# w_out as float32r through GpSimd transfers, the column mean straight from it, one operation to scale and centre, and log w in pairs, in a new order

## Chip, cores, metric

One core of one Trainium2 chip. The metric is the device time of one launch in microseconds (us), median over runs. The kernel before takes 151.41 us (three runs, 151.08 to 151.83). Where two kernels are compared, the ratio is the mean time of one kernel's fast runs over the mean of the other's fast runs of the same rounds, with a 95% interval; so it is not quite the ratio of the medians quoted beside it. A run counts as slow when it is over 1.5% above the fastest of the same kernel, and is then left out of the ratio, though not out of the median. "Loss" below is (ratio - 1) times the median of the kernel before in those rounds.

## The reference, cut

```python
for t in range(S):                       # attention: batch 4, 8 heads, 768 tokens, 48 wide
    cur = einsum('bhd,bhe->bhde', u * k[t], v[t])
    y[t] = einsum('bhd,bhde->bhe', r[t], state + cur)
    state = w[t][..., None] * state + einsum('bhd,bhe->bhde', k[t], v[t])
x = y.reshape(3072, 384)
h = x @ w_in                             # 384 x 1024
solu = h * softmax(h)
ln = (solu - mean(solu)) / sqrt(var(solu) + 1e-6) * g_ln
out = ln @ w_out                         # 1024 x 384
```

The mean of the layer norm is folded into the weights: with w = g * w_out (row by row), `(solu - mean) @ w` equals `solu @ (w - column mean of w)`. So w_out is scaled by g and centred once, at the start. That set-up is what the change is about.

## The kernel before

The sequence is cut into 24 units of 128 tokens. Every engine executes its own instructions strictly in the order of one list of words. A word is a step, a unit (or block) number and, where there is a choice, an engine: a = ACT (ScalarE), v = DVE (VectorE), g = GpSimd. The words used below: `ldw`, `ldk`, `ldr`, `ldv` load a unit (192 KB each, in pieces of 192 B); `ldwin`, `ldwout` load the weights; `lw` is log w, `cum` its cumulative sums, `kp`, `kt`, `kr`, `M`, `m` lead to the scores, `dg`, `dv` to the diagonal term, `Y`, `y` the attention output, `X`, `xT` its transpose; `H` is x @ w_in (h_ps), `e` the exponential, `he` = h * e, `hq` its square, `Oa`, `Ob` the product with w_out (o_ps). The set-up has `gw` (scale w_out by g), `mean`, and `wt` (centre); `dm` is a warm-up matmul.

```python
wout_f = consts.tile([128, KF, DM], F32)                       # KF = 8 blocks of 128 x 384
def load_w_out(half):                                          # ldwout: on the SyncE queue
    part = slice(half * KF // 2, (half + 1) * KF // 2)
    sp.dma_start(out=wout_f[:, part, :], in_=wout_v[:, part, :])
...
def setup_gain(f, engine):                                     # gw
    if engine is act:
        act.activation(out=gw[:, f, :], in_=wout_f[:, f, :], func=COPY, scale=gr[:, f:f + 1])
    else:
        engine.tensor_scalar(out=gw[:, f, :], in0=wout_f[:, f, :], scalar1=gr[:, f:f + 1], scalar2=None, op0=MULT)

def setup_mean():                                              # mean: eight bf16 matmuls
    for f in range(KF):
        pe.matmul(m_ps, lhsT=mean_w, rhs=gw[:, f, :], start=(f == 0), stop=(f == KF - 1))

def setup_w2(f, engine):                                       # wt: all eight on GpSimd
    engine.tensor_add(out=w2[:, f, :DM], in0=gw[:, f, :], in1=mean_sb)
...
def log_w(i):
    act.activation(out=L["lw"][:, :, :D], in_=L["w"], func=LN)
```

The list, from the last loads of w_out to the first output matmuls (cuts marked):

```
... m2v dv1v ldwout0 dm4 p2g Y1 q2g S1 y1v ldwout1 qa2 gw1a gw0a dm2 X1 xT0v xT1v dg2 H0 H1 ldw3 e0 st1 S0 dm13 ldv2 gw4v gw6v
gw3g he0 ldk3 gw5a ... gw7a ldr3 e1 ldk4 lw3 gw2g mean mean_sb:a vb2g ldw5 dv2g he1 Y2 ldr4 cum3 wt2g y2v exp3 lw4 et3 p3v
hq0a wt3g cum4 wt1g X2 dm0 wt0g ... wt4g kp3 S2 kt3 ... wt7g ... wt6g ldr6 Oa0 kp4 p4v exp5 wt5g ...
```

The softmax here doesn't subtract the row's maximum and nothing guards it: scores larger than these inputs give would overflow.

Of the kernel before, what the change touches and what calls it, by code (L numbers as in the profile page):

```python
# [14 lines left out]
SQUARE = mybir.ActivationFunctionType.Square  # L15
IDENTITY = mybir.ActivationFunctionType.Identity
# [8 lines left out]
dm5 dm3 dm18 dm1 ldw0 ldr0 small dm16 dm8 ldk0 lw0 ldw1 ldr1 cum0 exp0 et0 lw1 rows cum1 ldk1 p0g ldw2 kp0 exp1 ubc kt0 p1g kr0v ldr2 M0 ldk2 ldv0 et1  # L25
kp1 lw2 m0a q0g kt1 kr1v ldwin2 cum2 q1g sel0 dg0 exp2 M1 dm10 et2 vb0a kp2 m1a ldwin1 ldv1 kt2 win2a dg1 dv0g kr2v win1a vb1a Y0 y0v sel1 ldwin0 M2
win0a dm6 X0 m2v dv1v ldwout0 dm4 p2g Y1 q2g S1 y1v ldwout1 qa2 gw1a gw0a dm2 X1 xT0v xT1v dg2 H0 H1 ldw3 e0 st1 S0 dm13 ldv2 gw4v gw6v gw3g he0 ldk3
gw5a dm12 dm17 ldw4 st0 gw7a ldr3 e1 ldk4 lw3 gw2g mean mean_sb:a vb2g ldw5 dv2g he1 Y2 ldr4 cum3 wt2g y2v exp3 lw4 et3 p3v hq0a wt3g cum4 wt1g X2 dm0
wt0g ldk5 dm9 ldr5 exp4 lw5 ldw6 wt4g kp3 S2 kt3 ldv3 cum5 st2 ldw7 wt7g ldv4 et4 kr3a xT2v wt6g ldr6 Oa0 kp4 p4v exp5 wt5g M3 q3v et5 m3a kt4 kr4v
ldk6 Oa1 kp5 hq1a H2 M4 q4g kt5 Ob0 ldv5 sel3 ldw8 lw6 vb3a e2 dg3 kr5a dv3g m4v sq0a dg4 vb4g dv4g p5g vb5g Ob1 ldr7 M5 lw7 ldk7 Y3x ldv6 he2 m5v qm0  # L30
q5g p6g y3a cum6 X3 xT3v sq1v Y4 qm1 exp6 y4v H3 lv0 lv1 et6 ldr8 X4 hq2v ldk8 kp6 Oa2 dg5 o0a xT4a dv5g p7g sto0 ldw9 S4 e3 S3 st4 st3 q6g H4 Y5 vb6g
q7g ldr9 o1a he3 kt6 lw8 S5 Ob2 e4 ldk9 y5v cum7 ldr10 he4 kr6a st5 X5 hq3a sq2a exp7 M6 Oa4 ldv7 ldk10 ldr11 Oa3 qm2 m6v cum8 ldv8 qa6 et7 xT5a sto1
dg6 ldr12 ldk11 lv2 kp7 qa7 Ob3 dv6g exp8 p8g ldw10 p9v kt7 et8 o2a dg7 sq3g kp8 H5 qm3 q8g hq4a lv3 ldv9 e5 ldw11 Y6x kr7v ldv10 p10g M7 vb7g o3v Ob4
ldw12 kt8 m7v y6a q10g lw9 X6 sq4v he5 cum9 xT6a qm4 ldk12 exp9 kr8a dg8 et9 dv7g Y7 hq5g H6 e6 sto2 kp9 Oa5 ldw13 kt9 y7v lv4 X7 dg10 q9g Ob5 kr9a
he6 vb8g ldv11 ldk13 dv8g ldr13 sq5a o4a M8 ldw14 hq6g m8v S7 M9 qm5 vb10g xT7a p11g ldv12 m9v lv5 Oa6 H7 dg9 st7 lw10 Y8 o5a e7 cum10 vb9g ldw15
exp10 Ob6 y8v he7 sq6g X8 sto3 et10 dv9g S6 kp10 ldk14 xT8a lw12 S8 q11g H8 lw11 lw13 cum11 st8 e8 dv10g st6 Oa7 qm6 kt10 Y9x p12g exp11 hq7v kr10a
lv6 Ob7 y9a he8 M10 et11 S9 ldw16 sto4 o6a ldr14 X9 xT9a kp11 cum12 qa11 Oa8 ldr15 exp12 hq8g m10v p13g ldv13 vb11g ldk15 st9 H9 sq7v et12 qm7 kt11
q12g ldv14 lw14 ldr16 kp12 ldk16 lv7 e9 Y10x q13g sto5 y10a o7v ldk17 kr11v he9 cum13 exp13 ldv15 et13 dg11 kt12 kp13 Ob8 X10 sto6 M11 kr12a sq8g Oa9
qa12 ldk18 dv11g ldr17 dg13 M12 m12v kt13 ldw17 vb12g xT10a qm8 S10 m11a sel11 H10 kr13v M13 lw15 st10 ldv16 hq9a Y11x lv8 p15g e10 y11a m13v vb13g
sto7 o8a Ob9 dg12 p14g ldr18 ldv17 sq9v dv12g p16g X11 ldw18 cum14 xT11a S11 he10 Y12 H11 exp14 S12 qm9 st11 y12v lv9 et14 kp14 q14g dv13g st12 hq10g  # L40
o9a ldv18 e11 Y13 X12 cum15 xT12a ldr19 he11 exp15 kt14 Oa10 y13v sto8 hq11g kr14a vb15a q15g lw16 S13 H12 vb14g et15 ldk19 kp15 e12 dg14 X13 M14 p17g
dv14g kt15 ldw19 m14v xT13a he12 kr15a Ob10 H13 q17g sto9 hq12g sq10a st13 M15 Y14 m15v ldv19 qm10 lv10 vb16g Oa11 e13 lw18 q16g S14 lw17 o10v y14v
cum16 he13 ldw20 exp16 dg15 et16 hq13v Ob11 dv15g X14 kp16 Oa12 p18g sq11a p19g xT14a st14 qm11 lv11 H14 Ob12 o11a e14 cum17 q19g kt16 sq12v ldk20 Y15
sto10 he14 exp17 q18g qm12 Oa13 sto11 kr16a et17 hq14g y15v cum18 kp17 lv12 Ob13 M16 ldr20 ldk21 o12v exp18 dg17 X15 vb17g sq13v kt17 m16a et18 qm13
Oa14 xT15v kp18 kr17v sel16 lv13 H15 o13a lw19 dg16 e15 kt18 M17 dv17g dv16g vb19g ldv20 kr18v m17a lw20 Ob14 Y16 he15 M18 y16v sq14v S16 qm14 dg18
cum19 X16 ldv21 hq15g xT16v m18a exp19 Oa15 H16 ldw21 sel17 S15 dg19 lv14 o14a et19 kp19 Y17 lw21 ldr21 st16 e16 cum20 sel18 vb18g st15 y17v exp20
Ob15 sto12 ldk22 ldr22 X17 sto13 kt19 sq15v ldv22 xT17a he16 dv18g Y18 qm15 kr19a dv19g kp20 p20v y18v hq16g H17 M19 Oa16 lv15 X18 q20g Ob16 m19v o15a
e17 xT18a ldw22 lw22 p22g cum21 sq16v he17 qm16 p21g dg20 ldw23 hq17g ldv23 exp21 Y19 kt20 H18 vb20g ldr23 Oa17 lv16 y19v kp21 q21g kr20v o16a cum22
e18 he18 dv20g kt21 exp22 Ob17 kr21a M20 X19 sq17g S17 qm17 m20a lv17 kp22 qa21 sel20 lw23 S18 xT19v sto14 o17a st17 hq18g M21 Oa18 ldk23 m21v kt22
cum23 H19 sto15 st18 exp23 kr22v vb21a kp23 dg21 dv21g sto16 Y20 Y21 vb22a M22 q22g S19 e19 m22a vb23g y20v X20 p23v st19 he19 q23g Ob18 kt23 xT20a  # L50
sq18v H20 qm18 kr23a sel22 M23 y21v lv18 o18a X21 dg22 hq19v xT21v Oa19 m23a dv22v dg23 sel23 Y22 Ob19 y22v e20 he20 H21 dv23g Y23 sto17 X22 sq19a
Oa20 y23v X23 qm19 lv19 hq20g o19a xT22v e21 xT23v H22 e22 he21 Ob20 sto18 hq21g sq20a qm20 lv20 H23 he22 Oa21 Oa22 sto19 Ob21 e23 hq22g sq21a o20v
qm21 lv21 Ob22 he23 hq23v Oa23 sto20 sq22v sq23a qm22 o21v Ob23 sto21 lv22 qm23 Oc23 o22v sto22 lv23 dm14 oz23v dm15 o23a stz23 dm7 sto23 dm11 dm19
# [25 lines left out]
def kernel(  # L79
# [12 lines left out]
    nc = tc.nc  # L92
# [25 lines left out]
    def load(name, src):  # L118
        def stage(i):
            c, b = units[i]  # L120
            L = live[i]
            if name in "kr":

                if "k_and_r" not in L:
                    L["k_and_r"] = io.tile([C, 2, H, 64], F32, tag="kr_in", name="kr_in")
                t = L["k_and_r"][:, "kr".index(name)]
            else:
                t = io.tile([C, H, 64], F32, tag=name + "_in", name=name + "_in")
            L[name] = t[:, :, :D]
            sp.dma_start(out=L[name], in_=src[b, :, c * C:(c + 1) * C, :].rearrange("h t d -> t h d"))  # L130
        return stage
# [6 lines left out]
    wout_f = consts.tile([128, KF, DM], F32)  # L138
# [9 lines left out]
    def load_w_out(half):  # L148
        part = slice(half * KF // 2, (half + 1) * KF // 2)
        sp.dma_start(out=wout_f[:, part, :], in_=wout_v[:, part, :])  # L150
# [3 lines left out]
    nc.gpsimd.memset(uti_neg, -1.0)  # L154
    nc.gpsimd.affine_select(out=uti_neg, in_=uti_neg, compare_op=ALU.is_ge, fill=0.0, base=0,
                            pattern=[[1, C]], channel_multiplier=-1)
    uts = consts.tile([C, C], BF16)
    nc.gpsimd.memset(uts, 1.0)
    nc.gpsimd.affine_select(out=uts, in_=uts, compare_op=ALU.is_gt, fill=0.0, base=0,
                            pattern=[[1, C]], channel_multiplier=-1)  # L160
    ident = consts.tile([C, C], BF16)
    make_identity(nc, ident)
# [12 lines left out]
    lw_t = [consts.tile([C, H, 64], BF16, name=f"lw{j}") for j in range(NR)]  # L175
    kp_t = [consts.tile([C, 2, H, 64], BF16, name=f"kp{j}") for j in range(NR)]
    for j in range(NR):
        nc.vector.memset(lw_t[j][:, :, D:], 0.0)
        nc.vector.memset(kp_t[j][:, :, :, D:], 0.0)
# [7 lines left out]
    mean_w = consts.tile([128, 128], BF16)  # L187
    nc.vector.memset(mean_w, -1.0 / DF)
    nc.vector.memset(w2[:, :, DM:], 1.0 / RDF)

    ident_f = consts.tile([KF, KF], F32)
    make_identity(nc, ident_f)
# [4 lines left out]
    gw = consts.tile([128, KF, DM], BF16)  # L197
# [9 lines left out]
    def setup_rows_copy():  # L207
        dve.tensor_copy(out=u_bc.rearrange("t h d -> t (h d)"), in_=live[0]["u_ps"])
        dve.tensor_scalar(out=gr, in0=live[0]["g_ps"], scalar1=RDF, scalar2=None, op0=MULT)

# [15 lines left out]
    def setup_gain(f, engine):  # L226
        if engine is act:
            act.activation(out=gw[:, f, :], in_=wout_f[:, f, :], func=COPY, scale=gr[:, f:f + 1])
        else:
            engine.tensor_scalar(out=gw[:, f, :], in0=wout_f[:, f, :], scalar1=gr[:, f:f + 1], scalar2=None, op0=MULT)  # L230

    def setup_mean():
        m_ps = small.tile([128, DM], F32, tag="s", name="mean_ps")
        for f in range(KF):
            pe.matmul(m_ps, lhsT=mean_w, rhs=gw[:, f, :], start=(f == 0), stop=(f == KF - 1))
        live[0]["mean_ps"] = m_ps

    def setup_mean_copy(engine):
        copy(engine, mean_sb, live[0]["mean_ps"])

    def setup_w2(f, engine):
        engine.tensor_add(out=w2[:, f, :DM], in0=gw[:, f, :], in1=mean_sb)


    def log_w(i):
        L = live[i]
        L["lw"] = lw_t[i % NR]
        act.activation(out=L["lw"][:, :, :D], in_=L["w"], func=LN)
# [337 lines left out]
    def part(stage, j):  # L586
# [9 lines left out]
        ldw=load("w", w), ldk=load("k", k), ldr=load("r", r), ldv=load("v", v), ldwin=load_w_in, ldwout=load_w_out,  # L596
# [43 lines left out]
```

## Time and profile before

| | run profiled first | the same kernel again |
|---|---|---|
| time of that run | 156.91 us (slow) | 152.29 us (single run, state unknown) |
| first h_ps | 20.06 us | 20.01 us |
| first o_ps | 30.92 us | 29.67 us |
| first gw on w_out | 21.07 us | 19.80 us |
| first gw on its second half | 23.87 us | 21.88 us |
| matmuls from 85 to 105 us | 270 | 339 |

A line of the timeline: start, length, engine, operation, result <- inputs, size, how many, then in brackets the idle time before and what ended it. Two lines of its timeline (start, length, engine, operation, result <- inputs, size, how many, then in brackets the idle time before and what ended it):

```profile
19.80 1.12 ACT L71 ACTIVATE gw<-wout_f,gr 128x384 bf16<-128x384 f32 x2 [1.33 <-DMA wout_f<-in_moe_w_out_dram]
25.67 7.74 POOL L71 TENSOR_TENSOR w<-gw,mean_sb 128x384 bf16<-128x384 bf16 x8 [0.56 <-ACT mean_sb L71]
```

w_out kept ACT waiting for 1.33 us, and centring took GpSimd 7.74 us in one piece.

### The profile page before, as it was taken

Reading aid. Unit: us, or ns where it says so; the run is one execution under the profiler, and the core shown is the slowest. Engines: PE = TensorE matmul, PEld = TensorE weight load, DVE = VectorE, ACT = ScalarE, POOL = GpSimd, SP = SyncE. Lnnn points to the kernel's source line nnn. Section 1 sums busy time; section 2 is a strip of 40 time slices with the busy share of each in tenths; the row PEclk is TensorE's granted clock in tenths of the full one; section 3 lists DMA queues with packets and bytes.
Section 4 is the critical chain, followed back from the end, with each engine's and each line's share of the span. In section 5 each row is a group of like instructions: output and inputs, shape, how many; then the busy total and the mean of one; then the engine's idle time right before and its main releaser. Section 6 shows DMA issues by size and latency. Waiting matters only on the chain.

```text
span 155.2 us, 5295 instructions
## 1 busy us (share of the span) xinstructions
PE 140.4 (90%) x2156; PEld 109.7 (71%) x2156; DVE 129.4 (83%) x231; ACT 120.2 (77%) x232; POOL 123.1 (79%) x152
## 2 busy tenths in 40 slices
PE   6877897699999899999999799939999999999993
PEld 2344584477786787888788587737888778889771
DVE  7546738899998898999976989999889999998661
ACT  4456767989898979798989698829899888895742
POOL 3375965997999799999947999977799899976800
PEclk9999999999999999999999999999999999999999
DMA  4999997989999999899796999999989311011013
GB/s 95 201 185 301 380 303 152 213 160 190 208 202 184 204 229 187 194 205 233 154 205 157 218 217 200 228 250 180 215 196 211 100 51 55 2 55 55 18 62 127
DMA packets 104970, 27.09 MB, mean 175 GB/s; under 512 B 100329, under 2 KB 104562, under 8 KB 104946
## 3 DMA queue, kind: packets, MB, share of 16 engines
q1 hardware_dynamic: 104946, 26.75, 76.4%
q8 instruction: 17, 0.28, 0.7%
q14 instruction: 7, 0.06, 0.1%
HBM read 22.03 MB, written 4.72 MB: 172 GB/s over the span
## 4 chain that ended last, share of the span: by engine, by line
PE 50%; DMA 14%; DVE 10%; SPq 8%; POOL 8%; ACT 4%; issue 3%; POOLq 0%; DVEq 0%
PE o_ps L71 18%; PE h_ps L71 13%; SPq L71 8%; DMA kr_in<-in_k_dram 8%; DMA wout_f<-in_moe_w_out_dram 6%; POOL w L71 5%; PE kr_ps L71 5%; PE cum_ps L71 3%; PE m_ps L71 3%; PE y_ps L71 3%; PE s_ps L71 3%; DVE hq L71 3%; DVE kp L71 2%; PE x_ps L71 2%; DVE he L71 1%
## 5 line engine op out<-in xcount | busy, mean ns | idle before, releaser
L71 PE MATMUL o_ps<-w,he 128*128 128x385 bf16 (+2 forms) x200 | 42.2, 315 | 0.3 <-ACT sq L71 0.3
L71 PE MATMUL h_ps<-xT,win_sb 128*128 128x128 bf16 x576 | 36.0, 219 | 0.1
L71 PEld LDWEIGHTS <-win_sb 128*128 128x128 bf16 x576 | 32.9, 98 | 0.9 <-issue 0.2
L71 PE MATMUL o_ps<-inv_col,e 128*128 128x1 bf16 x192 | 31.1, 165 | 0.0
L71 DVE TENSOR_TENSOR he<-h_ps,e 128x1024 bf16<-128x1024 f32 x24 | 29.2, 1217 | 2.2 <-ACT e L71 2.2
L71 POOL TENSOR_TENSOR hq<-he 128x1024 bf16<-128x1024 bf16 x14 | 26.5, 1895 | 3.7 <-DVE he L71 2.4
L71 ACT ACTIVATE e<-h_ps 128x1024 bf16<-128x1024 f32 x24 | 24.5, 1021 | 6.2 <-PE h_ps L71 6.1
L71 PEld LDWEIGHTS <-he 128*128 128x128 bf16 x208 | 19.7, 96 | 10.5 <-issue 0.3
L71 ACT ACTIVATE cum_ps<-cum_ps 128x772 f32<-128x772 f32 (+1 forms) x24 | 19.2, 801 | 8.8 <-PE cum_ps L71 7.6
L71 DVE TENSOR_TENSOR kp<-cum_ps,kr_in 128x768 bf16<-128x768 f32 x24 | 22.7, 948 | 0.6 <-DMA kr_in<-in_r_dram 0.5
L71 POOL TENSOR_TENSOR q<-p,u_bc 128x384 bf16<-128x384 bf16 x23 | 22.0, 962 | 0.6 <-DVE p L71 0.5
L71 POOL TENSOR_TENSOR p<-kr_in 128x384 bf16<-128x384 f32 x18 | 17.9, 1001 | 5.4 <-DMA kr_in<-in_k_dram 5.4
L71 PEld LDWEIGHTS <-kp 128*128 128x128 bf16 x272 | 17.6, 102 | 4.4 <-DVE kp L71 2.3
L71 POOL TENSOR_TENSOR dv<-vb,dg 128x384 bf16<-128x384 bf16 x22 | 18.2, 830 | 2.3 <-ACT vb L71 1.5
L71 DVE TENSOR_TENSOR m<-m_ps,uts 128x1024 bf16<-128x1024 f32 x14 | 17.0, 1223 | 3.1 <-PE m_ps L71 3.0
L71 PEld LDWEIGHTS <-e 128*128 128x128 bf16 x192 | 18.3, 96 | 0.1
L71 PE MATMUL kr_ps<-ident,kp 128*128 128x128 bf16 x192 | 15.9, 230 | 1.4 <-DVE kp L71 1.4
L71 PEld LDWEIGHTS <-kr 64*128 64x128 bf16 (+1 forms) x272 | 10.7, 98 | 4.9 <-DVE kr L71 2.2
L71 ACT ACTIVATE lw<-w_in 128x384 bf16<-128x384 f32 x23 | 11.7, 523 | 2.7 <-DMA w_in<-in_w_dram 2.7
L71 ACT COPY kr<-kr_ps 128x1024 bf16<-128x1024 bf16 x13 | 13.2, 1014 | 0.5 <-PE kr_ps L71 0.4
L71 POOL TENSOR_SCALAR_AFFINE_SELECT m<-m 128x1024 bf16<-128x1024 bf16 x10 | 11.0, 1103 | 2.5 <-ACT m L71 2.4
L71 PE MATMUL cum_ps<-lw,uti_neg 128*128 128x384 bf16 x24 | 8.3, 347 | 4.8 <-DVE kp L71 3.3
(93 smaller groups left out, 284.3 us busy)
## 6 DMA issues: line engine op xcount, KB each, us to landing
w_in<-in_w_dram SPq DMA_DIRECT2D x24, 192.0 KB, 4.2
kr_in<-in_r_dram SPq DMA_DIRECT2D x24, 192.0 KB, 3.8
kr_in<-in_k_dram SPq DMA_DIRECT2D x24, 192.0 KB, 3.8
v_in<-in_v_dram SPq DMA_DIRECT2D x24, 192.0 KB, 3.8
out_dram<-o SPq DMA_DIRECT2D x23, 192.0 KB, 3.1
win_f<-in_moe_w_in_dram SPq DMA_DIRECT2D x3, 512.0 KB, 6.1
wout_f<-in_moe_w_out_dram SPq DMA_DIRECT2D x2, 768.0 KB, 8.8
out_dram<-o SPq DMA_DIRECT2D x2, 96.0 KB, 1.6
```

Source lines behind the costliest of these rows:

```text
L71: made = make(*args, **kwargs)
```

## The change

The intent: w_out comes early and by another engine's queue, so that nothing waits for it. It is read as float32r, so that TensorE can take the column mean straight from it without waiting for the scaled copy. Scaling and centring are one VectorE operation for four blocks; ACT and GpSimd share the other four. From unit 4 on w is loaded, and its log taken, for two units at once. The list was made anew.

```diff
-    wout_f = consts.tile([128, KF, DM], F32)
+    wout_f = consts.tile([128, KF, DM], F32R)
     def load_w_out(half):
-        sp.dma_start(out=wout_f[:, part, :], in_=wout_v[:, part, :])
+        pool.dma_start(out=wout_f[:, part, :], in_=wout_v[:, part, :])
...
+    def setup_gain_wide(engine):                     # gm: g spread to 128 columns
+        copy(engine, g_wide, gr.unsqueeze(2).to_broadcast([128, KF, 128]))
     def setup_gain(f, engine):
+        act.activation(out=w2[:, f, :DM], in_=wout_f[:, f, :].bitcast(F32), func=COPY, scale=gr[:, f:f + 1])
+    def setup_mean(half):
+            pe.matmul(live[0]["mean_ps"], lhsT=g_wide[:, f, :], rhs=wout_f[:, f, :], ...)
     def setup_w2(f, engine):
+        if "scaled" in live[f]:
+            engine.tensor_add(out=w2[:, f, :DM], in0=w2[:, f, :DM], in1=mean_sb)
+        else:
+            engine.scalar_tensor_tensor(out=w2[:, f, :DM], in0=wout_f[:, f, :].bitcast(F32), scalar=gr[:, f:f + 1], in1=mean_sb,
+                                        op0=MULT, op1=ALU.add)
...
-        act.activation(out=L["lw"][:, :, :D], in_=L["w"], func=LN)
+            act.activation(out=t.rearrange("t a h d -> t (a h) d")[:, :, :D],          # two units, from unit 4 on
+                           in_=live[i]["w2_in"].rearrange("t a h d -> t (a h) d")[:, :, :D], func=LN)
...
 ORDER: the whole list is new. Its start (iwout loads w_out), then its middle:
+... cum0 ldw1 ldk1 iwout0 exp0 ldr1 ldw2 iwout1 rows et0 kp0 lw1 cum1 ldk2 ubc p0g ...
+... vb1a dv1g lw3 dm16 H0 Y1 m2v vb2g dg2 cum3 e0 exp3 y1v p3g X1 he0 xT1a S1 hq0a H1 dv2g et3 kp3 kt3 st1 e1 Y2x kr3v M3 he1
+gw0a y2a m3v meanA X2 ldr4 S2 xT2a q3g vb3g meanB ldk4 ldr5 ldk5 gw3a gw6a mean_sb:a gw7a dg3 H2 dv3g wt3g ldw6 wt0g e2 st2
+wt2v Y3x S3 wt6g wt7g wt1v dm2 lw4 cum4 Oa0 p4g y3a wt4v X3 exp4 xT3a he2 cum5 q4g ldv4 exp5 wt5v Oa1 ... kp4 Ob0 ...
```

## The prediction

> **What bounds the kernel now.** I read the page first, engine totals and then the slices.
>
> ```profile
> PE 140.4 (90%) x2156; PEld 109.7 (71%) x2156; DVE 129.4 (83%) x231; ACT 120.2 (77%) x232; POOL 123.1 (79%) x152
> PE   6877897699999899999999799939999999999993
> DMA  4999997989999999899796999999989311011013
> ```
>
> TensorE is the busiest engine, and it falls short only in the first eight slices (31 us) and in one slice near 100 us. The DMA engines are nearly full from slice 2 to slice 31 (about 120 us): every byte moved earlier delays another one. Next, the table by stretches (columns: stretch, length, then busy us and instruction count of PE, weight loads, DVE, ACT, POOL; clock, DMA share, GB/s):
>
> ```profile
> 0.00:31.00 31.00, 23.93 (x212) 14.88 (x213) 20.46 (x62) 19.94 (x28) 19.68 (x32) 1.00 0.93 229
> 31.00:85.00 54.00, 52.90 (x898) 43.27 (x895) 48.88 (x77) 47.44 (x97) 47.88 (x66) 1.00 0.94 193
> 85.00:105.00 20.00, 16.23 (x270) 13.12 (x268) 18.32 (x25) 13.99 (x27) 19.02 (x20) 1.00 0.99 223
> 105.00:145.00 40.00, 39.75 (x683) 32.99 (x680) 36.67 (x61) 34.56 (x67) 33.89 (x36) 1.00 0.45 107
> 145.00:155.00 10.00, 7.56 (x108) 5.41 (x105) 5.03 (x8) 4.29 (x15) 2.60 (x2) 1.00 0.23 80
> ```
>
> Count matmuls rather than busy time. In the two dense stretches there are 898 + 683 in 94 us, 16.8 per us. At that pace the 212 of the first stretch, less about 20 warm-up ones, are 11.4 us of work, so 19.6 us of it are lost; 85 to 105 loses 20 - 270/16.8 = 3.9 us; the end loses 10 - 6.4 = 3.6 us. So only the start is worth a large change. Then the chain of waits, for what holds the start (start, length, what):
>
> ```profile
> 13.97 9.87 DMA wout_f<-in_moe_w_out_dram
> 23.87 1.12 ACT gw L71 x2
> 24.99 0.81 ACT e L71
> 25.80 0.51 ACT lw L71
> 26.31 0.38 ACT mean_sb L71
> 26.69 0.07 issue
> 26.75 7.75 POOL w L71 x8
> ```
>
> w_out lands at 23.9 us, is scaled by g (gw), averaged over its rows on TensorE, and GpSimd then spends 7.75 us centring the eight blocks one after another. The timeline has the first output matmul (o_ps) at 30.92 us, after four of the eight. Until then TensorE has little to do: 34 matmuls from 25 to 30 us.
>
> The loss near 100 us, in the timeline of that window, is of another kind:
>
> ```profile
> 98.25 4.09 DVE L71 TENSOR_TENSOR hq<-he 128x1024 bf16<-128x1024 bf16 x1
> 102.26 0.94 DVE L71 TENSOR_TENSOR kp<-cum_ps,kr_in 128x768 bf16<-128x768 f32 x1
> 103.26 0.34 PE L71 MATMUL cum_ps<-lw,uti_neg 128*128 128x384 bf16 x1 [2.71 <-DVE kp L71]
> ```
>
> The same hq operation takes 0.68 to 0.69 us at 40.9, 67.5 and 148.2 us. Here it took 4.09 us while GpSimd ran q, dv, p and p without a gap from 98.18 to 101.8 us, and TensorE then idled 2.71 us behind kp.
>
> **What the Trainium skill says.** "SBUF — State Buffer", section "SBUF: two separate sides": a VectorE operation with two SBUF inputs and a GpSimd operation that reads SBUF exclude each other for a whole instruction. The 4.09 us against 0.68 us agrees. "DMA: Bandwidth & Descriptors", section "SWDGE vs HWDGE vs iDMA": a float32r destination is a cast, which only a transfer issued by GpSimd can make. The kernel before has no such transfer. The same page, "Queues, rings and completion order": each DMA engine takes turns between its queues packet by packet. Before, all loads are on one queue, so its trace does not show this; but with 192-byte pieces on one queue and 1,536-byte pieces on the other, w_out should take most of the bandwidth while it runs. The same page, "Specifications", puts full rate at pieces of at least 512 B; the page's row with 100329 of 104970 packets under 512 B agrees, and so do 301 to 380 GB/s in slices 4 to 6, where w_in and w_out come in, against 200 in most others.
>
> **Part 1: w_out by GpSimd, early.** The two issues move from 13.3 us on the SyncE queue to GpSimd just after its constants (eight operations, 0.2 to 0.3 us each, so about 2.6 us; two issues of perhaps 1 us each, a guess, no such issue is in this trace). Its 1.57 MB at some 370 GB/s (slice 5) take 4.3 us of full DMA, so it should land at about 9 to 11 us in place of 23.9. It is not free: w, k, r of units 1 and 2, v and w_in come about 4.3 us later. The last w_in was used at 18.96 us, so it comes at 21 to 23 us and the first h_ps moves from 20.06 to 22 to 23 us. From unit 3 on the sum of bytes ahead is the same, one w load shorter, so r of unit 3 lands near 27 us (the DVE waited for it until 28.16).
>
> **Part 2: the mean straight from w_out.** g is spread to 128 columns (one ACT operation of 128x1024, about 1.0 us, like the 1.02 us copies), and eight matmuls of 384 columns in float32r replace eight in bf16 (1.67 us for the eight before). I take the same speed. No gw is needed ahead of the mean: 1.12 us + 0.81 + 0.51 leave the chain.
>
> **Part 3: scale and centre.** Before: eight gw (2 GpSimd at 1.25, 4 ACT at 0.61, 2 DVE at 0.42) and eight GpSimd additions at 0.97 (7.75 us). After: four ACT gw, four GpSimd additions (3.9 us), and four fused DVE operations, which I put at 0.55 us as other 384-wide DVE operations with two inputs. GpSimd loses 2.5 + 3.9 = 6.4 us at the start, DVE gains 2.2 - 0.8 = 1.4 us. From mean to first output: two GpSimd additions and two DVE operations side by side, 2 us in place of 3.9.
>
> **Part 4: w in pairs.** The group of lw has 0.523 us for 384 columns, that of cum_ps 0.801 us for 772: 0.278 us per 388 columns more. A pair is then 0.80 us, against 1.05 us for two. Ten pairs save 2.5 us of ACT, and ten issues on SyncE. The bytes stay. It loads and waits for two units at once, while DMA is full.
>
> **Part 5: a new order.** The lists also differ in which engine does what. By the means in the groups: ACT has hq +4 (1.07), kr -8 (1.01), m +2 (1.0), y +2 and xT +2 (0.48), vb -3 (0.51), w_in -1 (1.05), g spread +1 (1.0), lw -2.5 in all: about -3 us. GpSimd has hq -3 (1.9), bonus halves +3 (1.0), masks +2 (1.1), vb +3 (0.5), w_in +1 (1.3, estimated from vb), sums -2 (0.75), the issues +2 and part 3's -6.4: about -4 us. DVE has kr +8 (0.68), m -2 (1.22), hq -1 (0.68 free), y and xT -2 each (0.45), part 3's +1.4: about +1 us. TensorE gets two matmuls more for the bonus, nothing that counts. No total changes by over 4%, so the dense stretches hardly move.
>
> **The sum.** The new order puts more ahead of the first output: H of three units instead of two, and all of units 0 to 3, 239 matmuls against 196 by my count, 43/16.8 = 2.6 us of work. So the start breaks even if the first output comes at 30.9 + 2.6 = 33.5 us. My chain: r of unit 3 at 27, p and q on GpSimd to 29; kp at 28, kr at 29.2, scores, he, m to 31.5, dg 32.1, dv 33, two additions on GpSimd to 35 us. That is the late reading. The early one is that loads come a little sooner and waits overlap, 31.5 us. I take 32.7 us: a gain of 0.8 us. In the middle, of 3.9 us lost I give 1.0 us back, since 3 to 4 us fewer on ACT and GpSimd make blocking rarer; 0.2 us at the end. 151.4 - 2.0 = 149.4 us.
>
> **Rivals.** (a) The early w_out is as good as its intent: the whole 4 us from w_out's landing to the first output vanishes, TensorE fills from 26 us on, and the time is 146 to 147.5 us. For it: the chain above. Against: w_in and the units come later, and DMA is full in any case. (b) The port lock takes it back: four fused DVE operations with two SBUF inputs stand beside a run of four GpSimd additions, and one of them can be held up to 4 us, as hq was at 98.25; hq of unit 7 stays on DVE and again stands beside q, q and four halves on GpSimd. Then 151 to 153 us. For it: the 4.09 us. Against: it needs an unbroken GpSimd run at that moment. (c) The transfer was hidden anyway: the order of bytes decides the start, and time stays at 150.5 to 152. For it: the DMA row. (d) The cast or the float32r matmuls are slow: a slow cast at 3 to 4 times 4.3 us would still land by 20 us, ahead of the mean at about 28 us; four-pass matmuls would cost 8 x 0.5 = 4 us more on TensorE at a time when it is idle.
>
> **Range and chances.** (a) has about a third, my sum and (c) together half, (b) and (d) the rest. Range 146.2 to 152.4 us. 2% faster means under 148.4 us: 0.36. Slower by 2% means over 154.4 us, which takes (b) in both places: 0.09. Within 2%: 0.55.
>
> **What would show it.** Part 1 is right if gw or the mean waits for no transfer and the first h_ps starts at 22 to 23 us. The sum is right if the first o_ps is at 32 to 33.5 us with some 240 matmuls before it. Rival (b) shows as a fused operation or hq on DVE of 2 us and more; (d) as mean_ps matmuls above 0.33 us. If units 1 and 2 are not late, I have misjudged how queues share, and it is faster than I say. I am wrong altogether if the new order removes stalls after 35 us, which I can't read from the diff.

## The result

The changed kernel takes 158.09 us (four runs, 157.21 to 159.79, of which the last counts as slow) against 151.26 for the kernel before in the same rounds. The ratio is 1.0425, interval 1.037 to 1.048: slower, a loss of 6.4 us. Run once more beside other kernels (after_again) it took 158.3 us, ratio 1.0452, with a correct output.

The page of the changed kernel, engine totals and slices (40 slices of the span, busy tenths):

```profile
PE 137.6 (88%) x2158; PEld 108.2 (70%) x2158; DVE 128.7 (83%) x233; ACT 117.7 (76%) x223; POOL 120.1 (77%) x151
...
PE   6607958796999999999999999989999999999990
...
DMA  3999999997989999999978999999638111011112
```

The totals are within 3 us of those of before (in the profile of the run of 152.29 us, the "before" of this document: 138.6, 127.7, 119.7 and 122.9 us for PE, DVE, ACT, POOL), so the loss is no added work. TensorE has an empty slice at 8 to 12 us and is full from about 39 us on. The stretches of 5 us from 20 to 40 us, of the kernel before and then of the changed one (columns: stretch, length, then busy us and instruction count of PE, weight loads, DVE, ACT, POOL; clock, DMA share, GB/s):

```profile
20.00:25.00 5.00, 4.95 (x69) 4.13 (x68) 3.93 (x8) 4.26 (x7) 3.55 (x4) 1.00 1.00 215
25.00:30.00 5.00, 3.25 (x47) 2.37 (x46) 4.73 (x9) 4.36 (x8) 4.44 (x6) 1.00 1.03 205
30.00:35.00 5.00, 4.40 (x71) 3.60 (x69) 4.97 (x8) 4.66 (x7) 5.00 (x6) 1.00 0.98 191
35.00:40.00 5.00, 4.76 (x88) 3.73 (x86) 4.83 (x9) 3.92 (x13) 4.84 (x8) 1.00 1.02 201
```

```profile
20.00:25.00 5.00, 3.69 (x53) 2.58 (x54) 4.64 (x8) 3.51 (x5) 4.10 (x5) 1.00 1.12 233
25.00:30.00 5.00, 3.81 (x70) 3.38 (x67) 4.21 (x8) 3.76 (x5) 3.60 (x5) 1.00 0.99 197
30.00:35.00 5.00, 4.57 (x70) 3.90 (x66) 4.71 (x7) 4.18 (x9) 1.55 (x2) 1.00 1.03 206
35.00:40.00 5.00, 3.59 (x40) 2.22 (x38) 5.00 (x7) 4.09 (x7) 4.92 (x6) 1.00 0.82 158
```

Before, VectorE is full from 25 to 40 us (4.73 to 4.97 of 5 us), so it paces that stretch with GpSimd. In the changed kernel GpSimd is busy for only 1.55 us of 30 to 35, and from 35 to 40 TensorE does 40 matmuls in place of 88 while VectorE is full.

To see where the loss arises I counted each kind of matmul in the trace by time, and weighted it by what it takes in a dense stretch (an estimate: 0.057 us for h_ps, 0.094 for the mean of the two kinds of o_ps, 0.03 to 0.07 for the others). By 25 us the kernel before has done 9.9 us of such work and the changed one 6.1; by 40 us it is 23.3 against 17.2, by 85 us 75.2 against 69.6, by 140 us 139.9 against 134.3. So nearly the whole loss is there by 40 us, over half of it by 25 us, and it does not grow after that. The difference at 40 us, 6.1, is called "lag at 40 us" below and is given for each experiment. It serves to compare kernels, and is too large as a time: by these weights the kernel before does 51.9 us of work in the 45 us from 40 to 85. A plain count has 286 matmuls by 40 us against 365; 79 fewer are, at the 17 per us of a dense stretch, some 4.6 us. The two profiled runs themselves are 4.9 us apart (157.21 and 152.29 us). A plain count puts the other kernels in much the same order.

The chain of waits of the changed kernel (start, length, what) shows two pieces of it:

```profile
3.22 8.53 DMA w_in<-in_w_dram
...
32.63 1.02 ACT w L72 x2
33.65 0.39 ACT mean_sb L72
34.04 0.02 issue
34.06 2.91 DVE w L72 x3
36.98 1.15 DVE he L72
```

First, w of unit 1 takes until 11.75 us to land. The timelines, before and changed:

```profile
6.78 0.52 ACT L71 ACTIVATE lw<-w_in 128x384 bf16<-128x384 f32 x1 [0.90 <-DMA w_in<-in_w_dram]
```

```profile
11.77 0.52 ACT L72 ACTIVATE lw<-w_in 128x384 bf16<-128x384 f32 x1 [6.01 <-DMA w_in<-in_w_dram]
12.35 0.48 PE L72 MATMUL cum_ps<-lw,uti_neg 128*128 128x384 bf16 x1 [5.84 <-ACT lw L72]
```

Log w of unit 1 is 5.0 us later, TensorE is idle for 5.84 us, and the first h_ps starts at 24.01 us in place of 20.01. Second, the centring, on VectorE and GpSimd:

```profile
34.06 2.91 DVE L72 SCALAR_TENSOR_TENSOR w<-wout_f,gr,mean_sb 128x384 bf16<-128x384 f32 x3 [0.29 <-ACT mean_sb L72]
```

```profile
33.45 0.83 POOL L72 TENSOR_TENSOR dv<-vb,dg 128x384 bf16<-128x384 bf16 x1 [4.05 <-DVE dg L72]
34.24 4.22 POOL L72 TENSOR_TENSOR w<-w,mean_sb 128x384 bf16<-128x384 bf16 x4
```

GpSimd stands idle for 4.05 us behind VectorE, and then both centre at once: 0.97 us for each fused operation, 1.06 for each addition. The next he starts only at 36.90 us, and the first o_ps at 36.69 (29.67 before).

**Theories.** A: the early transfer of w_out takes the DMA away from the first units. B: centring on VectorE costs more than its own time, since VectorE paces this stretch and the two engines hold each other up. Rivals: the pairs of w, the float32r transfer or mean, the clock, or the new list itself.

### The profile page after: what moved, and what is told of

It is laid out like the page before. It is cut to its first block, busy times and chain, and to the rows that moved or that the text cites. A ratio compares the mean times of both kernels' runs of the same rounds, so it can differ in the third digit from the quotient of the medians.

```text
span 155.5 us, 5296 instructions
## 1 busy us (share of the span) xinstructions
PE 137.6 (88%) x2158; PEld 108.2 (70%) x2158; DVE 128.7 (83%) x233; ACT 117.7 (76%) x223; POOL 120.1 (77%) x151
## 3 DMA queue, kind: packets, MB, share of 16 engines
q0 software_dynamic: 1056, 1.57, 3.5%
## 4 chain that ended last, share of the span: by engine, by line
PE 67%; DVE 15%; DMA 5%; ACT 4%; issue 2%; POOL 2%; SPq 1%; DVEq 0%; ACTq 0%
PE o_ps L72 21%; PE h_ps L72 16%; PE kr_ps L72 7%; DMA w_in<-in_w_dram 5%; PE cum_ps L72 5%; PE y_ps L72 5%; PE m_ps L72 5%; DVE he L72 3%; PE s_ps L72 3%; PE x_ps L72 3%; DVE dv L72 2%; DVE w L72 2%; DVE m L72 2%; DVE y L72 1%; ACT e L72 1%
## 5 line engine op out<-in xcount | busy, mean ns | idle before, releaser
L72 PEld LDWEIGHTS <-win_sb 128*128 128x128 bf16 x576 | 32.7, 98 | 2.1 <-DVE he L72 1.0
L72 POOL TENSOR_TENSOR p<-kr_in 128x384 bf16<-128x384 f32 x19 | 19.6, 1036 | 10.5 <-DMA kr_in<-in_r_dram 10.5
L72 POOL TENSOR_TENSOR hq<-he 128x1024 bf16<-128x1024 bf16 x11 | 21.3, 1933 | 4.6 <-DVE qm L72 3.4
L72 DVE COPY kr<-kr_ps 128x1024 bf16<-128x1024 bf16 x19 | 13.0, 685 | 8.3 <-PE kr_ps L72 8.1
L72 PEld LDWEIGHTS <-kp 128*128 128x128 bf16 x272 | 17.2, 100 | 3.3 <-DVE kp L72 1.2
L72 DVE TENSOR_TENSOR m<-m_ps,uts 128x1024 bf16<-128x1024 f32 x12 | 14.6, 1217 | 1.4 <-PE m_ps L72 1.4
L72 PE MATMUL kr_ps<-ident,kp 128*128 128x128 bf16 x192 | 15.0, 225 | 0.7 <-DVE kp L72 0.7
L72 ACT ACTIVATE lw<-w_in 128x768 bf16<-128x768 f32 (+1 forms) x13 | 10.0, 769 | 6.0 <-DMA w_in<-in_w_dram 6.0
L72 POOL TENSOR_SCALAR_AFFINE_SELECT m<-m 128x1024 bf16<-128x1024 bf16 x12 | 13.1, 1090 | 1.9 <-ACT m L72 1.6
```

Of the source, the lines that this page charges most:

```text
L72: made = make(*args, **kwargs)
```

## The experiments

Eighteen runs were made; every output agreed with the reference. The first is the kernel before itself, for a profile of an undisturbed run.

> The kernel before, unchanged, for a profile in the fast state: the one at hand was a slow run (156.91 us against 151.3 for the others, clock 1.0). If the 4.09 us hq and the 2.71 us idle of TensorE near 100 us were part of what made that run slow, they are gone here and the span is about 149.7 us; if they are in every run, hq of unit 7 takes some 4 us again.

It took 152.29 us; its profile is the "before" of this document. The main runs in one table:

| run | median us | ratio (95%) | first h_ps | first o_ps | lag at 40 us |
|---|---|---|---|---|---|
| before_again | 152.29 | | 20.01 | 29.67 | 0 |
| changed kernel | 158.09 | 1.0425 (1.037-1.048) | 24.01 | 36.69 | 6.1 |
| before_wout_early_gp | 155.01 | 1.0235 (1.0195-1.0275) | 24.15 | 34.21 | 4.4 |
| before_centre_half_dve | 154.98 | 1.0224 (1.0166-1.0282) | 20.02 | 31.66 | 2.9 |
| before_early_and_centre | 159.24 | 1.0496 (1.0455-1.0537) | 24.76 | 37.63 | 9.6 |
| after_wout_late | 157.32 | 1.0299 (1.0235-1.0362) | 21.75 | 35.31 | 4.2 |
| new_setup_old_order | 156.72 | 1.0365 (1.0309-1.0422) | 19.32 | 33.92 | 5.4 |
| new_setup_no_fused | 152.64 | 1.0106 (1.0043-1.017) | 19.86 | 29.86 | 1.1 |
| new_setup_no_fused_pairs | 153.4 | 1.0136 (1.0089-1.0184) | 19.68 | 30.64 | 1.9 |
| after_no_fused_wout_late | 156.02 | 1.03 (1.0231-1.037) | 21.59 | 34.09 | 4.0 |
| after_no_fused_e0_first | 157.8 | 1.0406 (1.0358-1.0454) | 21.29 | 35.12 | 5.9 |

### A: the early transfer, alone

```diff
 kernel before, list:
-... m2v dv1v ldwout0 dm4 ... S1 y1v ldwout1 qa2
+... cum1 ldk1 ldwout0 ldwout1 p0g ...
 and for before_wout_early_gp also:
-        sp.dma_start(out=wout_f[:, part, :], in_=wout_v[:, part, :])
+        pool.dma_start(out=wout_f[:, part, :], in_=wout_v[:, part, :])
```

> The kernel before with the two w_out loads moved forward to just after k of unit 1, still on the SyncE queue, nothing else changed. Theory A (bytes moved early delay the first units, and that is most of the loss): w, k, r of unit 2, v and w_in land some 4 us later, the first h_ps moves from 20 to 23-24 us, the time rises by 2 to 4 us to 153 to 155. Rival (the order of bytes is not it, the new order of instructions is): within 1 us of 151.3, the first o_ps not later than 31 us.

> As the run before it, but the two w_out loads are issued by GpSimd (float32, no cast), so that they have a queue of their own beside SyncE's. Theory A with queue sharing (w_out's 1,536-byte pieces get more than their share): w of unit 1 lands near 11.8 us as in the changed kernel and the time is 1 to 2 us above that of the run on SyncE, 154 to 157. If the queue makes no difference, the two are within 0.7 us.

By GpSimd: 155.01 us, ratio 1.0235, a loss of 3.6 us. Its timeline has the late log w of unit 1:

```profile
10.94 0.52 ACT L71 ACTIVATE lw<-w_in 128x384 bf16<-128x384 f32 x1 [5.16 <-DMA w_in<-in_w_dram]
```

On the SyncE queue the four runs were 154.12, 155.0, 157.81 and 158.14 us; two of them are over 1.5% above the fastest, so count as slow. The two fast ones are 2.8 and 3.7 us above the kernel before (151.33), and the first h_ps is at 23.9 us. Here it is w of unit 2 that comes late (its log at 14.37 us in place of 9.36), since w of unit 1 stands ahead of w_out on the queue. So early bytes cost about as much on either queue: it is the DMA that is short, not the issuing engine. In both profiles the granted clock was halved for part of 8 to 25 us. To tell that from the late loads, twelve more warm-up matmuls went ahead of the sums of unit 1:

```diff
-... exp0 et0 lw1 rows cum1 ldk1 ldwout0 ldwout1 ...
+... exp0 et0 lw1 rows dm20 dm21 ... dm31 cum1 ldk1 ldwout0 ldwout1 ...
```

> before_wout_early_gp (155.0 us, clock at half from 8 to 25 us) with twelve warm-up matmuls in TensorE's idle stretch at 6 to 11 us. If the halved clock is a part of what the early w_out costs, the matmuls run at full pace from 12 us and the time falls by 0.5 to 1.5 us; if only the late loads count, it stays at 155.0 within 0.4 us.

It took 155.59 us, ratio 1.0212 (1.0118 to 1.0307), with a mean clock of 0.989 against 0.944, and the first h_ps at 23.9 us. The median is 0.6 us above the run without them, a little more than allowed for "only the late loads count", and one of its runs took 153.45 us. Clearer are the four runs of before_wout_early_gp itself: with a mean clock of 0.944, 0.944, 0.999 and 1.0 they took 155.1, 155.01, 155.01 and 154.96 us. So the clock is not the cause; the loads are. In the profile of the changed kernel (157.21 us) the clock is no matter either: its mean is 0.995. Now the same undone in the changed kernel:

```diff
-... ldk1 iwout0 exp0 ldr1 ldw2 iwout1 rows ...
-... ldv0 p2g ldwin2 ...
+... ldv0 p2g iwout0 iwout1 ldwin2 ...
```

> The changed kernel with its two w_out transfers issued by GpSimd after p of unit 2, at about 13 us, nothing else changed. Theory A: w of unit 1 lands at about 7 us, the first h_ps at about 20 us and the first o_ps at 32 to 33 us in place of 36.7; the time falls from 158.1 to 153.5-155. Rival (the new order, or the fused and paired operations, lose it): less than 1 us is gained.

157.32 us, ratio 1.0299: 4.5 us of loss in place of 6.4. The ratio rests on two runs (155.82 and 156.14 us); the other two, 158.5 and 159.0, count as slow, and are in the median. Log w of unit 1 is back at 6.95 us, but the first h_ps came at 21.75 us, not the expected 20, and the time is above the expected 153.5 to 155. Moving w_out back returns about 1.9 us, where the transfer alone had cost 3.6. A is real and is not the whole of it.

### The pairs of w

`ldw` and `lw` of the changed kernel back to one unit each, all else kept:

```diff
-... ldw4 ... lw4 ... ldw6 ... lw6 ...                       (each for two units)
+... ldw4 ldw5 ... lw4 lw5 ... ldw6 ldw7 ... lw6 lw7 ...     (each for one)
```

> The changed kernel with w and its log one unit at a time (both units' loads and logs where the pair's stood), all else as changed. Theory: the pairs are worth little, ten ACT operations of 0.25 us saved, so the time stays at 158 within 1 us, and ACT is busier by 2.3 to 2.5 us. Rival (a pair of 384 KB that must land whole delays the units): faster by over 1 us than the changed kernel.

157.72 us, ratio 1.0434 (1.0346 to 1.0522): the same. A pair's log takes 0.83 us against 0.52 for one, so ACT does save (117.7 us busy against 118.7), and it is worth nothing to the time. The pairs are neither cause nor gain.

### Centring earlier in the new list: four misses

If the idle 4 us of GpSimd and the late centring are the matter, then centring early should help. after_w2_early takes the mean ahead of the first h_ps and spreads the `wt` over the idle places (its sibling also has w_out late):

```diff
-... S0 ldv3 dm11 y0v X0 dg1 dm1 ldw4 xT0v st0 vb1a dv1g lw3 dm16 H0 ... (mean, gw, wt as before, after S2)
+... S0 meanA ldv3 y0v X0 dg1 dm1 ldw4 xT0v meanB st0 vb1a dv1g lw3 mean_sb:a gw0a gw3a H0 ... he0 wt1v wt2v ...
```

> The same moves of mean, centring and first output, with w_out early as in the changed kernel. Theory A + D: first h_ps at 24 us as in the changed kernel, first o_ps at about 30-31 us in place of 36.7, the time 154.5-156.5 against 158.1. Rival as before: no gain.

> The changed kernel with w_out issued after p of unit 2 (as in after_wout_late) and besides with the mean, gw, the centring and the first output moved ahead of unit 3's steps in the order (TensorE: mean before the first h_ps, first output after the second h_ps; the other engines likewise). Theory D (the new order makes the first output wait for unit 3): the first o_ps moves from 35.3 to about 30 us and the time falls by 2 to 4 us against after_wout_late (157.3), to 153.5-155. Rival (steady stalls of the new order after 40 us lose it): the first o_ps is early, but the time stays within 1 us of after_wout_late.

Both missed: 159.49 us (1.0492) and 159.74 us (1.0497). The mean stood ahead of the first h_ps and ran while TensorE was hardly used (1.63 us for its first four matmuls against 0.97 in the changed kernel), so h_ps itself was late: 27.19 us in the first of them. (The profiles of both are of slow runs, 160.91 and 193.59 us.) The test was badly built and says little on B. The second attempt puts the mean between `S1` and `H1`, four additions into GpSimd's idle time and the fused operations in twos:

```diff
+... lw3 gw0a gw1a gw2a gw3a dm16 H0 ... S1 meanA meanB hq0a H1 mean_sb:a ... vb3g wt0g wt1g wt2g wt3g ...
+... H2 Oa0 dv3g ldw6 e2 st2 wt4v wt5v ... he2 wt6v wt7v ...
```

> The changed kernel once more, as the base for the two runs after it on the same chip: 157 to 159 us, first o_ps at 36.7 us.

> The changed kernel with the work on w_out moved into idle stretches that its trace shows, nothing else: the four ACT scalings into ACT's 2.03 us before the first exp, the mean between s and h_ps of unit 1, four GpSimd centrings (blocks 0 to 3) into GpSimd's 4.05 us before dv of unit 3, the fused DVE ones for blocks 4 to 7, the first output right after the third h_ps. Theory D (the burst of w_out work between 32 and 38 us is the second part of the loss): first o_ps at 34 to 35 us in place of 36.7, the time 1.5 to 2.5 us below after_again, about 156. Rival (steady stalls later): less than 0.7 us. A fused DVE operation away from the GpSimd run takes 0.55 us in place of 0.97 if the port lock made it long; about 0.9 if that is its own length.

> Both causes taken away: the same moves with w_out issued after p of unit 2. If loads (A, about 2 us here) and burst (D, about 2 us) add up: 153.5 to 154.5 us. If they hide each other: about 156.

158.28 us (1.0452), no better than the changed kernel repeated beside it (after_again, 158.3), though the first o_ps came at 34.73 us, 3 us earlier than in after_again (37.70, itself 1.0 us later than in the first profile of that kernel). With w_out late it was 156.71 us (1.0356). The GpSimd additions took 0.84 us each with VectorE out of the way, and the fused pair took 2.28 us beside other GpSimd work and again held the next he. An earlier first output is no gain by itself.

### B: centring on VectorE, in the old list

The changed set-up in the list of before: w_out issued after `dv0g` (about 15 us), the mean straight from it, blocks 2, 3, 4 and 6 fused on VectorE, w singly.

```diff
 list of before, program text of the changed kernel:
-... dg1 dv0g ... dv1v ldwout0 ... y1v ldwout1 ... gw4v gw6v gw3g ... lw3 gw2g mean ... wt2g ... wt3g ... wt4g ... wt6g
+... dg1 dv0g iwout0 iwout1 ... m1a gm:a ... lw3 meanA meanB ... wt2v ... wt3v ... wt4v ... wt6v
```

> The new set-up (w_out rounded by GpSimd transfers, the mean straight from it, four fused DVE operations, four GpSimd ones) in the order of the kernel before, w_out issued by GpSimd after dv of unit 0 at about 15 us, w one unit at a time. If the new operations are sound and only the early transfer and the new order lose: 150.5 to 152 us, first o_ps at 28 to 29.5 us. If the new set-up itself costs (cast transfer, float32r, port lock): over 153 us.

156.72 us, ratio 1.0365, although no transfer is early here (first h_ps at 19.32 us). The fused operations in the view of that tile (shortest/median/longest in ns):

```profile
L72 DVE SCALAR_TENSOR_TENSOR w<-wout_f,gr,mean_sb x4: 604/1096/1197, 27.0 to 33.0; 128x384 bf16<-128x384 f32 x4
```

604 ns is the last one, when GpSimd stood idle; the median of the four, three of them beside GpSimd's additions, is 1096 ns. Two kernels tell the fused operation from the rest of the new set-up. In the first, all `gw` go to ACT and all `wt` to GpSimd, and `hq0` moves back behind the last `gw`; the second has the pairs as well:

```diff
-... gw4v gw6v gw3g ... wt2v ... wt3v ... wt4v ... wt6v
+... gw3a gw2a ... gw4a gw5a ... gw6a ... gw7a, and wt0g to wt7g
```

> The changed kernel's code for set-up (w_out by GpSimd at about 15 us, mean straight from it) in the order of the kernel before, w loaded singly, all eight gw on ACT and all eight centring additions on GpSimd: no fused operation on VectorE. Theory B (the fused operations sit on VectorE while it is the critical engine at 25 to 40 us, and that is what the run with the old order lost): 150.5 to 152.5 us, first output matmul near 29.5 to 31 us. Rival (the cast transfer, the float32r mean or the issue on GpSimd costs it): over 154 us, as the run with the fused operations in the old order had 156.7.

> The same with w and its log in pairs from unit 4 on. If the pairs are neutral, as undoing them in the changed kernel said: within 0.7 us of the same kernel without pairs, so 150 to 152.5 us. If waiting for two loads at once costs something where the loads are not late: over 1 us more.

152.64 us (1.0106) and 153.4 us (1.0136). Taking the four operations off VectorE returns 3.9 us (5.5 of loss against 1.6). The rest of the new set-up, the cast transfer, the float32r mean and the scaling by ACT alone, costs about 1.6 us in this list (0.7 to 2.6 by the interval). The first run came out 0.1 us above its expected range and the second 0.9 us above. The pairs differ from single loads by 0.3% with overlapping intervals.

And B alone, in the kernel before:

```diff
-... wt2g ... wt3g ... wt4g ... wt6g
+... wt2v ... wt3v ... wt4v ... wt6v      (a plain bf16 addition, on VectorE in place of GpSimd)
```

> The kernel before with one thing changed: four of the eight centring additions are on VectorE in place of GpSimd, the two engines side by side. Theory B: plus 2 to 4 us, 153.5 to 155.5 us, with the VectorE additions at about 1 us each beside GpSimd's and kp of the next unit later by their sum. Rival (VectorE has room there, since GpSimd's chain is halved): at most plus 0.7 us, or faster by up to 1 us.

154.98 us, ratio 1.0224, a loss of 3.4 us, as theory B expected. Its timeline on GpSimd, VectorE and TensorE:

```profile
25.57 4.06 POOL L71 TENSOR_TENSOR w<-gw,mean_sb 128x384 bf16<-128x384 bf16 x4 [0.30 <-ACT mean_sb L71]
```

```profile
27.80 2.04 DVE L71 TENSOR_TENSOR w<-gw,mean_sb 128x384 bf16<-128x384 bf16 x2
29.77 0.94 DVE L71 TENSOR_TENSOR kp<-cum_ps,kr_in 128x768 bf16<-128x768 f32 x1
...
31.44 0.34 DVE L71 TENSOR_TENSOR w<-gw,mean_sb 128x384 bf16<-128x384 bf16 x1
```

```profile
30.77 0.62 PE L71 MATMUL kr_ps<-ident,kp 128*128 128x128 bf16 x8 [2.52 <-DVE kp L71]
```

The same addition takes 0.34 us alone and 1.02 us beside GpSimd's. It pushes kp of unit 3 from 27.79 to 29.77 us, and TensorE idles 2.52 us behind that kp, while GpSimd, done early, waits 3.56 us for VectorE: work was taken from an engine that now waits and given to the one that TensorE waits for. How much of the 3.4 us is the hold-up between the two engines, and how much VectorE's own work (four additions at 0.34 us are 1.4 us), no run tells apart. In this profile the granted clock is 0.68 from 30 to 35 us, behind that idle time; but the runs with a mean clock of 0.978 took 155.3 and 155.27 us, and those with 0.955 and 0.944 only 153.91 and 154.69, so a lower clock does not go with more loss.

### Both together, and what the new list costs

> Both suspected causes added to the kernel before and nothing else: w_out issued early by GpSimd, and four centring additions on VectorE. Alone they cost plus 3.6 and plus 3.3 us. If they add up, 158 to 159 us, as slow as the changed kernel, and the order need not be blamed for it; if the second hides behind the first (VectorE waits for late loads in any case), 155 to 156.5 us, and part of the changed kernel's loss must come from its order.

The kernel before with A and B and nothing else: 159.24 us, ratio 1.0496, a loss of 7.5 us. Singly they cost 3.6 and 3.4. They add up, and they are enough to make the kernel before as slow as the changed one. Now the reverse, both taken out of the changed kernel (w_out after `p2g`, all `gw` on ACT, all `wt` on GpSimd):

```diff
-... ldk1 iwout0 ... ldw2 iwout1 ... lw3 dm16 H0 ... wt3g ... wt0g ... wt2v ... wt6g wt7g wt1v ... wt4v ... wt5v
+... p2g iwout0 iwout1 ... lw3 gw0a gw1a gw2a gw3a dm16 H0 ... xT2a gw4a gw5a gw6a gw7a ... wt0g wt1g wt2g wt3g ... H2 Oa0 dv3g wt4g wt5g wt6g wt7g
```

> The changed kernel in its own order with both suspected causes taken out: w_out issued after p of unit 2, all gw on ACT, all eight centring additions on GpSimd in its idle time, nothing of it on VectorE. If late loads (A) and centring on VectorE (B) are the whole of it: 151 to 153.5 us. If the new order itself costs something as well: 154.5 to 157 us, with the lag already there when the first output matmul starts.

156.02 us, ratio 1.03. This kernel and new_setup_no_fused_pairs (1.0136) have the same program text and differ in the list alone, so the new list, as it stands in this run, costs 1.6%, some 2.5 us (the intervals of the two ratios do not overlap). The timelines show what differs: kp, the start of a unit's scores, of units 3, 4 and 5, with the old list and then with the new:

```profile
28.75 0.95 DVE L72 TENSOR_TENSOR kp<-cum_ps,kr_in 128x768 bf16<-128x768 f32 x1
30.46 0.96 DVE L72 TENSOR_TENSOR kp<-cum_ps,kr_in 128x768 bf16<-128x768 f32 x1
34.30 0.95 DVE L72 TENSOR_TENSOR kp<-cum_ps,kr_in 128x768 bf16<-128x768 f32 x1
```

```profile
28.71 0.95 DVE L72 TENSOR_TENSOR kp<-cum_ps,kr_in 128x768 bf16<-128x768 f32 x1
...
38.46 0.95 DVE L72 TENSOR_TENSOR kp<-cum_ps,kr_in 128x768 bf16<-128x768 f32 x1
...
39.39 0.95 DVE L72 TENSOR_TENSOR kp<-cum_ps,kr_in 128x768 bf16<-128x768 f32 x1
```

The old list has units 3 and 4 under way together; the new one leads unit 3 alone, and units 4 and 5 come 8 and 5 us later. That this is why it loses is argued, not shown. One guess at a cause was tried (C): in the new list `cum3` stands between `H0` and `H1` and takes the second of the two large accumulators, and `lw3`, which waited 5.23 us for w of unit 3 here, stands ahead of `e0` on ACT.

```diff
-... lw3 gw0a gw1a gw2a gw3a dm16 H0 Y1 m2v vb2g dg2 cum3 e0 exp3 ... S1 meanA meanB hq0a H1 mean_sb:a dv2g et3 kp3
+... dm16 H0 Y1 m2v vb2g dg2 e0 ... S1 lw3 gw0a gw1a gw2a gw3a meanA meanB hq0a H1 mean_sb:a dv2g cum3 exp3 et3 kp3
```

> The run with both suspects taken out of the changed kernel, with one more edit in its order: log w and the cumulative sums of unit 3, and four gw, now come behind e of unit 0, so that ACT does not hold e back (it waited 5.23 us for w of unit 3 there and started e at 26.46 us) and the two h_ps of units 0 and 1 follow each other with no cum_ps between them, which takes the second of the two large accumulators in the changed order. Theory C (the new order's own loss is this separation): 152 to 154 us, second h_ps before 25 us against 28.77. Rival (the loss of the new order lies elsewhere): 155.5 us or more.

157.8 us, ratio 1.0406: it got worse. The second h_ps came earlier (26.50 us against 28.77), e of unit 0 at 23.81 against 26.46, but kp of unit 3 slipped to 30.13 us behind its later sums and TensorE idled 2.72 us for it. C fell. Which words of the new list cost its 2.5 us stays open.

None of the kernels beat the kernel before; the nearest, new_setup_no_fused, is 1.06% behind it.

## Why the prediction was wrong, step by step

- **What bounds the start.** The prediction read w_out's landing at 23.9 us as the thing that holds the start. Its page was of a slow run; in the undisturbed one the second half of w_out was in use at 21.88 us in place of 23.87 and the first o_ps came at 29.67 in place of 30.92, and 85 to 105 us has 339 matmuls, not 270. So there was less to win at the one place, and of the "3.9 us lost" near 100 us, of which it gave 1.0 back, nothing was there to give.
- **Part 1.** The mechanism was right: the early w_out makes the units' loads later, w of unit 1 by 5.0 us (about 4.3 predicted). The size was short: first h_ps at 22 to 23 us was predicted, 24.01 measured. The prediction let the last w_in alone set it; the chain of waits runs from w of unit 1. "From unit 3 on the sum of bytes ahead is the same" held: GpSimd started on r of unit 3 at 26.30 us (27 predicted), and kp of unit 3 came at 27.82 (28 predicted, 27.79 before). The step that failed is what was drawn from it, that the start is gated by the loads of unit 3, so that what units 0 to 2 lose costs nothing more. TensorE was 51 matmuls behind by 25 us (119 against 170) and did not make them up. Alone the early transfer costs 3.6 us.
- **Part 2** held for TensorE and the transfer. The float32r mean took 0.97 and 0.95 us for its two halves of four matmuls, in the changed kernel, against 1.46 for eight bf16 ones before; the transfer with its cast landed in time. Rival (d) is refuted for the matmuls: one takes 0.34 us, just over the sign of 0.33 that it was given and far from four passes. But "1.12 us + 0.81 + 0.51 leave the chain" did not come true: the new list has `gw3a gw6a` ahead of `mean_sb:a` on ACT, and the chain shows 1.02 us of them there.
- **Part 3** is the second step that failed. The prediction put a fused operation at 0.55 us; alone it is 0.60, but three took 2.91 us and the fourth 0.85, 3.76 in place of 2.2. It then counted VectorE's part as side by side with GpSimd's, in place of asking which engine paces that stretch: VectorE, at 4.7 to 5.0 of 5 us. Its rival (b) saw the port lock, though as one hold-up of 4 us rather than a surcharge on every operation: the sign that it named, a fused operation or hq on VectorE of 2 us and more, did not appear (1.26 and 0.80 us at most). The Trainium skill's "SBUF — State Buffer", section "SBUF: two separate sides", says that the two kinds of operation exclude each other for a whole instruction; the trace agrees: the same addition took 0.34 us on VectorE alone and 0.91 on GpSimd (median of the eight before the change), and about 1.02 on each beside the other, far nearer the sum than either's own time.
- **Part 4** was right about the pair (0.80 us estimated, 0.83 measured) and wrong to hope for time from it.
- **Part 5** held for the totals, with some luck: its own terms add up to -4.0 us on ACT and +1.9 on VectorE where it wrote -3 and +1, and -2.0 and +1.0 were measured. None moved by over 3 us, and the dense stretches hardly changed (691 matmuls from 105 to 145 us against 692). It did not see that a list can cost 2.5 us with equal totals.
- **The sum.** "The start breaks even if the first output comes at 33.5 us" used the right count (46 matmuls more before it, 43 estimated), but the first o_ps came at 36.69, past even the late reading of 35, and what follows it counts too: 40 matmuls from 35 to 40 us against 88. That late chain was nearly right up to dv of unit 3 (33 predicted, 33.45 measured); after it the mean came at 34.04 and each addition took 1.06 us. The 32.7 that the prediction took instead had no run for it. Rival (a), the full gain, is refuted. Rival (c), the transfer hidden anyway, was half right: hidden it was, and moving it made others visible.

How the 6.4 us divide inside the changed kernel is settled only in part. A and B are each shown alone and together in the old list, and together suffice. In the new list, taking A away returned 1.9 us and taking B away as well returned nothing more in my test, which had put four `gw` ahead of e on ACT; there the new list's own cost takes their place. One pair of runs in the new list differs in B alone, after_fill_idle_wout_late with four fused operations on VectorE (1.0356) and after_no_fused_wout_late without (1.03): some 0.8 us, with overlapping intervals. So in the new list B is not shown to cost what it costs in the old one. The three costs hide behind each other, and their sum (3.6, 3.4 and 2.5, with 1.6 to 2.1 for the rest of the set-up) is more than the whole.

## What to carry to other kernels

Ask of an early transfer whose bytes it displaces: here the DMA was full from 2 us on, and w_out's lead came straight out of the load of unit 1. Before moving work to a "faster" engine, look at which engine has no idle time in that very stretch, and time the operation beside the neighbour it will run with, not alone. And take the profile of an undisturbed run before looking for what a change can win.

## What the Trainium skill lacked or had wrong

- "SBUF — State Buffer", "SBUF: two separate sides": the lock agrees, but the page gives no cost for a run of short operations on both engines. Here a 128x384 bf16 addition on VectorE went from 0.34 to 1.02 us and GpSimd's from 0.91 to about 1.02; the fused scale-and-add went from 0.60 to a median of 1.01 to 1.10 us in runs beside four GpSimd additions (1.35 at most in any kernel). Sharing eight additions between both saved GpSimd half its time and cost the program 3.4 us.
- "DMA: Bandwidth & Descriptors", "Queues, rings and completion order": engines take turns between queues packet by packet, but the page does not say what share a transfer of large pieces gets beside one of small ones. Here 1.57 MB on GpSimd's queue put a 192 KB load of 192 B pieces on the other queue back by 5.0 us, and the same transfer on the same queue moved the first h_ps just as far (23.9 us against 24.2).
- No page that I found gives the rate of float32r matmuls: eight of 384 columns took 1.64 us in one run at full clock (after_fill_idle), against 1.46 for eight in bf16.
- "TensorE: Matmul & The Clock Gate", "Part 1: The HAM clock gate (the "warmup" mystery)": two states, half and full, a third (13/16) only where three or more cores are busy, and a warning that the clock was once seen stuck at a quarter; none is 0.65. One run (of after_w2_early_wout_late) had a granted clock of 0.50 to 0.65 from 14 us and of 0.65 from 25 us to its end, on one core with TensorE fully busy for most of that time, and took 193.59 us against 158 to 160 for its other runs.
